# Part of w_ch and two row blocks of w_in decoded in another stage of a three-part kernel (attention, gated layer, rotation layer)

## The chip, the cores and the metric

One core of one Trainium2 chip. The metric is the device time of one execution in microseconds (us). The engines are TensorE (PE; its weight loads are PEld), VectorE (DVE), ScalarE (ACT), GpSimd (POOL) and SyncE (SP), which here issues all DMA transfers.

## The reference

Attention over 4 batches, 12 heads, 448 positions and 64 features a head, with the heads mixed before and after the softmax. Its output x, 4 x 448 x 768, goes through two layers:

```python
# layer one
h = gelu_tanh(x @ w_in)                       # 768 -> 1024
u, v = h[..., :512], h[..., 512:]
v_n = (v - mean(v)) / sqrt(var(v) + 1e-6) * g_ln
v_s = einsum('ts,bsd->btd', w_sg, v_n) + b_sg[None, :, None]
x = x + (u * v_s) @ w_out                     # 512 -> 768
# layer two
theta = x @ w_theta                           # 768 -> 768
y = einsum('ts,bsd->btd', w_tok_r, x * cos(theta)) + einsum('ts,bsd->btd', w_tok_i, x * sin(theta))
u = x + y
out = u + maximum(u @ w_ch, 0)                # 768 -> 768
```

## The kernel before

All matrix products of the layers are made of three: an fp32 operand is split into a high part (a ScalarE cast to the reduced type `fp32r`) and a low part (the operand minus that cast), and high x high, high x low and low x high are added up in PSUM. Activations are split when they are made. The weights w_in, w_out, w_theta, w_tok and w_ch lie in memory as 64-bit floats; the kernel decodes them from the two 32-bit words of each number into a high and a low part. That is the work that the change moves about.

**The decode.** One piece is 128 rows and 256 (or 192) columns. `Dense.decode` makes six steps of it: load the raw words; two ScalarE copies and two VectorE bit operations (`words`, L597 to L602); a VectorE mask (`value`, L608); a ScalarE cast and a VectorE product (`high`, L613, L614); a VectorE subtraction and a GpSimd addition (`low`, L620, L621); a store to a scratch tensor in memory (`store`, L627), unless the result goes straight into tiles. Pieces are made in two ways:

- `extra`: a list handed to `attention`, spread evenly over its 180 blocks: the v half of w_in (columns 512 to 1023, 12 pieces) and the u half of the first KE row blocks (2 pieces each), all stored to `win_d` and loaded again by `load_win`.
- `d.jobs`: a list worked off by `d.tick`, a software pipeline over the list: each tick makes one step of each of the pieces under way, so that a full tick is one piece's worth of work; the last step of a piece (its store) is seven ticks behind its load. The list is: the u half of w_in's remaining row blocks, straight into tiles (two pieces a block); w_out (12 pieces, tiles); w_theta (18), w_tok (14) and the first KC row blocks of w_ch (3 each), all by way of memory. Some ticks run beside the end of attention (`at(-6 + KE + i, d.tick)`), the others behind units of layer one, as many as the tables TV, TU, TG and TO say for the units `v_chunk`, `u_half`, `gate` and `out` of each batch. What is left runs in `rest` of layer two.

The row blocks of w_ch from KC on are decoded in layer two, in tiles of 128 x 384, without scratch memory: `load_wch` brings the raw words, `words_wch` makes a ScalarE copy and four VectorE operations, `split_wch` a ScalarE cast (high part), and two VectorE operations (low part).

**The order of the work.** Every engine works in order, and the order of emission is written out by hand. Attention is a loop over blocks of 10 positions x 12 heads (score matmuls, a layout change by DMA, the head mix on TensorE, a row maximum on VectorE, exp on ScalarE, split and normalisation on GpSimd and VectorE, the second head mix, its split, then the product with v and the transposed store to `xT`). v of each batch is scaled and split beside some of the blocks (L181, L184, L188). Behind the loop layers one and two are a list of units, each with work put before (`pre`) and behind it (`post`). For each batch layer one runs `v_chunk` (4 or 3), `out` of the batch before, `u_half` (4), `gate` (4). The first four `v_chunk` units run beside the end of attention. In layer two `theta` units (two a chunk of 128 positions, with `angles` and `rotate` behind them) come first, then six `tok` units of batch 0, then for each batch theta of the next, six `ch` units of the one before and six `tok`. `tok0` is the index of the first `tok` unit. The chunk (1, 0) is computed ahead of `tok0`, and its rotation is held back to the last `tok` units of batch 0.

A `tok` unit accumulates in one of eight PSUM buffers, VectorE adds x (L1117), ScalarE casts the sum to `uh`, and the difference makes `ul`; both feed the `ch` units.

Of the kernel before, what the change touches and what calls it, by code (L numbers as in the profile page):

```python
# [7 lines left out]
F32R = mybir.dt.float32r  # L8
# [475 lines left out]
NO2 = 3  # L484
TV = ((), (2, 2, 2), (1, 1, 1, 1), (1, 1, 1))
TU = ((2, 1, 1, 1), (2, 1, 1, 1), (2, 1, 1, 1), (1, 1, 1, 2))
TG = ((1, 0, 1, 0), (1, 0, 1, 0), (1, 0, 1, 0), (1, 1, 0, 0))
TO = ((1, 1, 1, 1, 1, 1), (1, 0, 1, 0, 1, 0), (1, 0, 1, 0, 1, 0), (0, 1, 1, 0, 0, 0))
KC = 3
KE = 1  # L490
MAGIC = 12582912.0
INV2PI = 1.0 / (2.0 * math.pi)
C1 = 6.28125
# [5 lines left out]
class Dense:  # L499
# [64 lines left out]
    def scratch(self, dram):  # L564
# [3 lines left out]
        self.wtok_d = t("wtok_d", 2 * S, S)  # L568
        self.wch_d = t("wch_d", 128 * KC, DM)

# [89 lines left out]
def moe1(d, left, right):  # L660

    tc, nc, io = d.tc, d.nc, d.io
# [4 lines left out]
    def start():  # L667
# [14 lines left out]
        pair = lambda pool, n, tag: [d.pools[pool].tile([128, n], F32R, tag=f"{tag}_{i}", name=tag) for i in range(2)]  # L682
        for k in range(KE, KD):
            def tiles(k=k):
                win[k, 0] = pair("win", HF, f"win{k}_0")
                return win[k, 0]
            d.jobs += d.decode_tiles(io["w_in"], slice(128 * k, 128 * k + 128), 0, HF, tiles)
        d.jobs += [None]
        for k in range(KF):
            def tiles(k=k):  # L690
# [4 lines left out]
                   + d.decode_all(io["w_tok"], 0, S, d.wtok_d)  # L695
                   + d.decode_all(io["w_ch"], 0, DM, d.wch_d, 128 * KC))

# [166 lines left out]
    for b in range(B + 1):  # L864
# [13 lines left out]
        if b < B:  # L878
            g0[b] = len(d.units)
            for f in range(KF):  # L880
                i = U(gate, b, f)
# [8 lines left out]
    for b in range(B):  # L890
# [3 lines left out]
        for c in range(nv):  # L894
            i = o0[b - 1][0] + 1 + c if b else u0[0] + c // 2
# [3 lines left out]
        if b + 1 < B:  # L899
            i = u0[b] + KF  # L900
# [9 lines left out]
    for b in range(B):  # L910
# [4 lines left out]
        for f in range(KF):  # L915
            ticks[u0[b] + f] = TU[b][f]
            ticks[g0[b] + f] = TG[b][f]
        for m in range(KD):
            ticks[o0[b][m]] = TO[b][m]
    for i, n in ticks.items():  # L920
# [4 lines left out]
    def at(s, fn, *a):  # L925
        tail.setdefault(s, []).append(lambda: fn(*a))
# [4 lines left out]
    for k in range(KD):  # L931
        at(-6 + k // 2, load_win, k, 1)
    for k in range(KE):
        at(-3, load_win, k, 0)
    for i in range(17 - 2 * KE):
        at(-6 + KE + i, d.tick)
    for c in range(4):
# [7 lines left out]
def moe2(d, left, win_es, last_u, m1_left):  # L945
    tc, nc, io = d.tc, d.nc, d.io
    wth, wch, wtok, z, x2, st, ut, res = ({} for _ in range(8))
# [23 lines left out]
    def load_wch(k, half):  # L971
        if k < KC:
            wch[k, half] = d.load_pair(d.pools["wch"], d.wch_d, slice(128 * k, 128 * k + 128),
                                       slice(384 * half, 384 * half + 384), f"wch{k}_{half}")
            return
        raw = d.pools["wch"].tile([128, 384, 2], U32, tag=f"wch{k}_{half}", name="wchraw")
        src = io["w_ch"][128 * k:128 * k + 128, 384 * half:384 * half + 384]
        nc.sync.dma_start(out=raw.rearrange("p n w -> p (n w)"), in_=src.bitcast(U32))
        wch[k, half] = raw

    def words_wch(k, half):
        raw = wch[k, half]
        a, p = (d.pools["t2"].tile([128, 384], F32, tag=f"zz{i}", name=f"ch{i}") for i in range(2))
        nc.scalar.activation(out=p, in_=raw[:, :, 1].bitcast(F32), func=AF.Copy, scale=2.0 ** -112)
        au, pu = a.bitcast(U32), p.bitcast(U32)
        nc.vector.tensor_scalar(out=au, in0=pu, scalar1=3, scalar2=0x7FFFFFF8,
                                op0=ALU.logical_shift_left, op1=ALU.bitwise_and)
        nc.vector.scalar_tensor_tensor(out=au, in0=pu, scalar=0x80000000, in1=au,
                                       op0=ALU.bitwise_and, op1=ALU.bitwise_or)
        nc.vector.tensor_scalar(out=pu, in0=au, scalar1=0xFF800000, scalar2=None, op0=ALU.bitwise_and)  # L990
        nc.vector.tensor_tensor(out=p, in0=p, in1=raw[:, :, 0], op=ALU.mult)
        st["ch", k, half] = a, p

    def split_wch(k, half):
        a, p = st.pop(("ch", k, half))
        t = d.pools["wch"].tile([128, 2, 384], F32R, tag=f"wch{k}_{half}", name="wch")
        d.cast(t[:, 0], a)
        d.rest(nc.vector, a, a, t[:, 0])
        nc.vector.scalar_tensor_tensor(out=t[:, 1], in0=p, scalar=2.0 ** -52, in1=a, op0=ALU.mult, op1=ALU.add)
        wch[k, half] = t[:, 0], t[:, 1]  # L1000
# [103 lines left out]
    def tok(b, k):  # L1104
        if k == 0:
            ut[b] = ([], [])
        fs = slice(128 * k, 128 * k + 128)
        ps = d.ps()
        terms = []
        for c in (0, 1, 2, 3) if b % 2 == 0 else (3, 0, 1, 2):  # L1110
            for ri in range(2 if c < 3 else 1):
                zh, zl = (z[(b, c, ri, hl) if c < 3 else (b, 3, hl)][:, fs] for hl in "hl")
                wh, wl = wtok[(c, ri) if c < 3 else 3]
                terms += [(zh, wh), (zh, wl), (zl, wh)]
        d.mm(ps[:, :S], terms)
        x = res.pop(("x", b, k))
        nc.vector.tensor_tensor(out=x, in0=ps[:, :S], in1=x, op=ALU.add)  # L1117
        uh, ul = (d.pools["x"].tile([128, 512], F32R, tag=f"x{i}{k}", name="u") for i in range(2))
        uh, ul = uh[:, :S], ul[:, :S]
        d.cast(uh, x)  # L1120
        d.rest(nc.gpsimd, ul, x, uh)
        ut[b][0].append(uh)
        ut[b][1].append(ul)

# [23 lines left out]
        for half in range(2):  # L1148
            d.post(last_u + 1 + k, load_wth, k, half)
    d.pre(first, rest)  # L1150
    chunks = []
    def theta_units(b, cs):
        for c in cs:
            chunks.append((b, c, len(d.units)))
            for half in range(2):
                U(theta, b, c, half)

    for b in range(B):
        cs = (0, 1, 2, 3) if b % 2 == 0 else (0, 1, 2)
        theta_units(b, cs if b != 1 else cs[1:])  # L1160
        if b == 0:
            theta_units(1, (0,))
        if b:
            for m in range(KD):
                U(ch, b - 1, m)
        k0 = len(d.units)
        if b == 0:
            tok0 = k0
        for k in range(KD):
            U(tok, b, k)  # L1170
        for k in range(KD):
            d.pre(k0 + k - 1, load_res, b, k)
# [10 lines left out]
    for i in range(7):  # L1183
        d.pre(first + 1 + i, load_wtok, i)
    words = [(k, half) for half in range(2) for k in range(KC, KD)]
    for j, kh in enumerate(words):
        d.pre(tok0 - 3 + j, load_wch, *kh)
        d.post(tok0 + j, split_wch, *kh)
    for j, kh in enumerate(words):
        d.post(tok0 - 1 + j, words_wch, *kh)  # L1190
    for half in range(2):
        for k in range(KC):
            d.pre(tok0 + k + half, load_wch, k, half)
# [13 lines left out]
def build(tc, nc, io, out):  # L1207
    with tc.manual_schedule(), ExitStack() as top:
        dram = top.enter_context(tc.tile_pool(name="scratch", bufs=1, space=bass.MemoryType.DRAM))
        xT = dram.tile([DM, B * S], F32, name="xT")  # L1210
        x2T = dram.tile([DM, B * S], F32, name="x2T")
        d = Dense(tc, nc, io, xT, x2T, out)
        d.scratch(dram)
        right, left1, left2 = ExitStack(), ExitStack(), ExitStack()
        tail, win_es, last_u, end = moe1(d, left1, right)
        th_es = moe2(d, left2, win_es, last_u, left1)
        for i in range(4):
            tail.setdefault(-2 + 2 * i, []).append(d.step)
        jobs = d.decode_all(io["w_in"], HF, DFF, d.win_d)
        jobs += d.decode_all(io["w_in"], 0, HF, d.win_d, 128 * KE)  # L1220
        attention(tc, nc, io, xT, B, jobs, tail)
        while d.at < len(d.units):
            d.step()
        th_es.close()
        right.close()
        left2.close()
# [54 lines left out]
```

## Time and profile before

| | |
|---|---|
| median of 3 runs | 1026.55 us (1026.28 to 1028.11) |
| profiled execution | 1026.51 us, span of its instructions 1024.7 us |
| TensorE busy | 975.8 us, 95% of the span, granted clock 0.985 on average |
| TensorE weight loads | 742.4 us, 72% |
| VectorE busy | 784.0 us, 77% |
| ScalarE busy | 593.3 us, 58% |
| GpSimd busy | 483.6 us, 47% |

The columns of a busy table are the sum of an engine's busy time in a stretch, the number of its instructions in brackets, the clock granted to TensorE as a share of full speed, the busy share of the DMA engines and what they moved. In a timeline a row is: start, length, engine, line of the kernel, operation, output <- input, shapes, how many in a row, and in square brackets how long the engine was idle just before and who ended that. A row of waits is: who <- for whom, microseconds in total, how often, the longest.

### The profile page before, as it was taken

To read this page: it belongs to the slowest core of one execution; us is meant where nothing else is said; L and a number is where in the kernel's file an instruction comes from. 1 tells how busy PE (TensorE), PEld (TensorE's weight loads), DVE (VectorE), ACT (ScalarE), POOL (GpSimd) and SP (SyncE) were. 2 spreads that over 40 slices of the span, in tenths; PEclk is the share of its full clock that TensorE was granted. 3 is DMA by queue.
4 is the path that set the end of the run, shared out by engine and by line. 5 is a ranking of instruction groups with operands and counts; after the bars stand their busy time and mean duration, and the time that the engine had idled before them with its cause. 6 is when DMAs were issued, how large, how long until landed. Compare 5 with 4: busy or idle time off the path is not lost.

```text
span 1024.7 us, 21768 instructions
## 1 busy us (share of the span) xinstructions
PE 975.8 (95%) x7856; PEld 742.4 (72%) x7856; DVE 784.0 (77%) x1605; ACT 593.3 (58%) x1392; POOL 483.6 (47%) x653
## 2 busy tenths in 40 slices
PE   8889999999999999997998999999997899999998
PEld 3456565566656565576877888888987799999997
DVE  2999879988889888986999898984987825835511
ACT  5777788688877887765855646442552513513310
POOL 0694458655685557752312222222552643743623
PEclk9999999999999999998999999999999899999999
DMA  5557555654456445248534856679761031130121
GB/s 172 184 180 216 142 147 176 190 152 141 149 194 206 133 156 172 101 108 277 181 99 148 264 180 207 205 241 287 228 218 49 17 109 31 32 108 16 39 70 54
DMA packets 126905, 153.17 MB, mean 149 GB/s; under 512 B 26318, under 2 KB 113230, under 8 KB 126798
## 3 DMA queue, kind: packets, MB, share of 16 engines
q1 hardware_dynamic: 126798, 151.78, 47.4%
q8 instruction: 63, 1.03, 0.4%
q14 instruction: 44, 0.36, 0.1%
HBM read 82.73 MB, written 30.47 MB: 110 GB/s over the span
## 4 chain that ended last, share of the span: by engine, by line
PE 70%; DVE 17%; DMA 4%; ACT 3%; issue 3%; POOL 2%; SPq 1%; DVEq 0%; ACTq 0%; POOLq 0%
PE ps L562 39%; PE psB L226 10%; PE psA L206 6%; PE psD L332 5%; DVE pl L265 3%; PE psC L280 3%; PE psC L283 2%; PE psC L281 2%; DVE al L311 2%; DVE nmx L232 2%; DMA blk<-s 1%; DMA win<-win_d 1%; DVE dp L608 1%; DMA x2T<-xres 1%; DVE dp L614 1%
## 5 line engine op out<-in xcount | busy, mean ns | idle before, releaser
L258 POOL TENSOR_SCALAR ph<-e,rc 120x448 f16<-120x448 f32 x180 | 174.2, 968 | 145.3 <-DVE rc L253 94.6
L226 PE MATMUL psB<-blk,kpre 120*120 120x448 f32 x360 | 175.2, 569 | 5.1 <-DMA blk<-s 2.9
L232 DVE TENSOR_REDUCE nmx<-psB 120x1 f32<-120x448 f32 x180 | 111.2, 618 | 43.5 <-PE psB L226 42.7
L265 DVE SCALAR_TENSOR_TENSOR pl<-e,rc,ph 120x448 f16<-120x448 f32 x180 | 143.2, 796 | 0.0
L239 ACT ACTIVATE e<-psB,nmx 120x448 f32<-120x448 f32 x180 | 114.2, 634 | 36.7 <-DVE nmx L232 34.7
L311 DVE SCALAR_TENSOR_TENSOR al<-psC,ah 128x480 f16<-128x480 f32 x180 | 116.1, 645 | 7.6 <-ACT ah L305 7.0
L562 PE MATMUL ps<-wtok,z 128*128 128x448 f32 x504 | 104.3, 367 | 0.4 <-POOL z L558 0.4
L212 ACT ACTIVATE s<-psA 120x896 f32<-120x896 f32 (+1 forms) x90 | 82.4, 916 | 37.5 <-PE psA L206 36.0
L305 ACT ACTIVATE ah<-psC 128x480 f16<-128x480 f32 x180 | 103.1, 573 | 0.1
L562 PE MATMUL ps<-wth,x2s 128*128 128x384 f32 x504 | 96.3, 348 | 6.9 <-DVE xres L1117 4.2
L280 PE MATMUL psC<-wh,ph 120*128 120x120 f16 x720 | 96.9, 218 | 6.1 <-DVE rc L253 4.1
L562 PEld LDWEIGHTS ps<-wtok,z 128*128 128x128 f32 x504 | 94.5, 188 | 9.5 <-POOL z L558 0.8
L621 POOL TENSOR_TENSOR dh<-da,dp 128x256 fp32r<-128x256 f32 (+1 forms) x55 | 44.7, 813 | 119.8 <-DVE da L620 70.4
L280 PEld LDWEIGHTS <-ph 120*128 120x128 f16 x720 | 68.3, 98 | 42.5 <-POOL rc L247 18.3
L332 PEld LDWEIGHTS <-ah 128*128 128x128 f16 x1536 | 76.6, 99 | 30.6 <-issue 30.6
L206 PE MATMUL psA<-k,q 64*120 64x448 f32 (+1 forms) x384 | 96.2, 580 | 1.0 <-ACT s L212 1.0
L562 PEld LDWEIGHTS ps<-wth,x2s 128*128 128x128 f32 x504 | 91.0, 195 | 8.3 <-DVE xres L1117 4.1
L281 PE MATMUL psC<-wl,ph 120*128 120x120 f16 x720 | 96.1, 217 | 0.0
L562 PE MATMUL ps<-u,wch 128*128 128x448 f32 x432 | 89.5, 367 | 0.0
L562 PEld LDWEIGHTS ps<-u,wch 128*128 128x128 f32 x432 | 81.1, 188 | 7.6
L558 POOL TENSOR_TENSOR z<-zz,z 128x384 fp32r<-128x384 f32 x56 | 61.9, 1125 | 47.0 <-ACT z L555 46.8
L332 PE MATMUL psD<-vh,ah 128*128 128x64 f16 x768 | 78.6, 195 | 0.0
(132 smaller groups left out, 2071.4 us busy)
## 6 DMA issues: line engine op xcount, KB each, us to landing
blk<-s SPq DMA_DIRECT2D x176, 210.0 KB
draw<-in_w_in SPq DMA_DIRECT2D x24, 256.0 KB
vraw<-in_vN SPq DMA_DIRECT2D x24, 256.0 KB
k<-in_kvT SPq DMA_DIRECT2D x24, 224.0 KB
vT<-in_kvT SPq DMA_DIRECT2D x12, 448.0 KB
xraw<-xT SPq DMA_DIRECT2D x24, 224.0 KB
xres<-xT SPq DMA_DIRECT2D x24, 224.0 KB
x2T<-xres SPq DMA_DIRECT2D x24, 224.0 KB
```

Of the source, the lines that this page charges most:

```text
L206: nc.tensor.matmul(ps[e][:n, :S], q[p, o:o + n], k[p], start=True, stop=True)
L226: nc.tensor.matmul(ps[:r, :S], kpre[:r, :r], sblk.pop(s)[:r], start=True, stop=True)
L232: nc.vector.tensor_reduce(out=m[:r], in_=mix[s][:r, :S], axis=AX.X, op=ALU.max, negate=True)
L239: nc.scalar.activation(out=e[:r], in_=mix.pop(s)[:r, :S], func=AF.Exp, bias=nmx.pop(s)[:r], accum_out=sm[:r])
L258: nc.gpsimd.tensor_scalar(out=p[:r], in0=ex[s][0][:r], scalar1=rec[s][:r], scalar2=0.0, op0=ALU.mult, op1=ALU.add)
L265: nc.vector.scalar_tensor_tensor(out=p[:r], in0=ex.pop(s)[0][:r], scalar=rec.pop(s)[:r], in1=ph[s][:r], op0=ALU.mult, op1=ALU.subtract)
L280: nc.tensor.matmul(ps[:, jc, :, :n], cols(a, jc), wh[:r, :, :n], start=(jc == 0), stop=False)
L281: nc.tensor.matmul(ps[:, jc, :, :n], cols(a, jc), wl[:r, :, :n], start=False, stop=False)
L305: nc.scalar.activation(out=at_view(s, at[b, t][0]), in_=src, func=AF.Copy, scale=2.0 ** -17)
L311: nc.vector.scalar_tensor_tensor(out=al, in0=src, scalar=2.0 ** -17, in1=ah, op0=ALU.mult, op1=ALU.subtract)
L332: nc.tensor.matmul(ps[:, o:o + 64], a[:, i0:i0 + 128], v[:, jc, 64 * e:64 * e + 64], start=(o == 0 and m == 0), stop=(o == 320 and m == le ...
L562: self.nc.tensor.matmul(ps, l, r, start=(i == 0), stop=(i == len(terms) - 1))
```

## The change

Two constants and three tables change, and the order of the work on w_ch in layer two:

- KE goes from 1 to 3: the u half of two more row blocks of w_in (4 pieces) is decoded beside attention's blocks, 18 pieces instead of 14, and goes by way of memory; the list `d.jobs` loses these 4 pieces, and 11 ticks instead of 15 run beside the end of attention. The three blocks are loaded at steps 1 to 3 behind attention's last block.
- KC goes from 3 to 4: one more row block of w_ch (3 pieces) is decoded in `d.jobs`; layer two decodes two row blocks, 4 tiles instead of 6, spread over the units from tok0 - 1 to tok0 + 5.
- TG and TO have four ticks more: behind the last `gate` of batch 0, behind `out` units of batches 2 and 3.
- In layer two the cast of w_ch's high part is emitted with the words, directly behind them, and no longer with the split one unit later.
- u's low part is computed by VectorE and no longer by GpSimd.

```diff
-TG = ((1, 0, 1, 0), (1, 0, 1, 0), (1, 0, 1, 0), (1, 1, 0, 0))
-TO = ((1, 1, 1, 1, 1, 1), (1, 0, 1, 0, 1, 0), (1, 0, 1, 0, 1, 0), (0, 1, 1, 0, 0, 0))
-KC = 3
-KE = 1
+TG = ((1, 0, 1, 1), (1, 0, 1, 0), (1, 0, 1, 0), (1, 1, 0, 0))
+TO = ((1, 1, 1, 1, 1, 1), (1, 0, 1, 0, 1, 0), (1, 0, 1, 0, 1, 1), (0, 1, 1, 1, 1, 0))
+KC = 4
+KE = 3
...
     for k in range(KE):
-        at(-3, load_win, k, 0)
+        at(1 + k, load_win, k, 0)
     for i in range(17 - 2 * KE):
         at(-6 + KE + i, d.tick)
...
         nc.vector.tensor_tensor(out=p, in0=p, in1=raw[:, :, 0], op=ALU.mult)
-        st["ch", k, half] = a, p
-
-    def split_wch(k, half):
-        a, p = st.pop(("ch", k, half))
         t = d.pools["wch"].tile([128, 2, 384], F32R, tag=f"wch{k}_{half}", name="wch")
         d.cast(t[:, 0], a)
+        st["ch", k, half] = a, p, t
+
+    def split_wch(k, half):
+        a, p, t = st.pop(("ch", k, half))
         d.rest(nc.vector, a, a, t[:, 0])
...
         d.cast(uh, x)
-        d.rest(nc.gpsimd, ul, x, uh)
+        d.rest(nc.vector, ul, x, uh)
...
     for j, kh in enumerate(words):
-        d.pre(tok0 - 3 + j, load_wch, *kh)
-        d.post(tok0 + j, split_wch, *kh)
-    for j, kh in enumerate(words):
-        d.post(tok0 - 1 + j, words_wch, *kh)
+        i = tok0 - 1 + (3 * j + 1) // 2
+        d.pre(i - 2, load_wch, *kh)
+        d.post(i + 1, split_wch, *kh)
+        late_words.append((i, kh))
+    for i, kh in late_words:
+        d.post(i, words_wch, *kh)
```

## Rows read from the trace of the kernel before

**Rows 1.** Busy time by stage; stretch, length, then the engines.
```profile
20.00:468.00 448.00, 430.56 (x5047) 261.71 (x5047) 394.08 (x823) 354.34 (x861) 282.80 (x452) 1.00 0.54 163
...
480.00:550.00 70.00, 62.98 (x431) 52.62 (x430) 66.75 (x154) 47.79 (x122) 16.98 (x20) 0.96 0.44 136
...
550.00:700.00 150.00, 148.03 (x684) 127.99 (x682) 132.60 (x305) 77.36 (x180) 34.76 (x41) 0.99 0.69 224
762.00:800.00 38.00, 28.18 (x139) 25.62 (x137) 29.50 (x52) 10.64 (x22) 9.13 (x9) 0.89 0.11 33
...
830.00:1025.00 195.00, 191.12 (x987) 177.91 (x985) 85.50 (x139) 48.44 (x98) 83.18 (x75) 1.00 0.18 56
```

**Rows 2.** Whom TensorE waited for, from 440 us to the end.
```profile
PE ps L562 <- POOL wout L621: 3.1, 1, 3.1
...
PE ps L562 <- DVE x L558: 2.1, 2, 1.4
...
PE psT L345 <- ACT xi L336: 1.7, 1, 1.7
```

**Rows 3.** Timeline of the first tok stage, 764 to 802 us.
```profile
766.83 0.62 DVE L1117 TENSOR_TENSOR xres<-ps,xres 128x448 f32<-128x448 f32 x1
...
768.45 0.56 ACT L555 ACTIVATE u<-xres 128x448 fp32r<-128x448 f32 x1
...
783.57 0.62 DVE L1117 TENSOR_TENSOR xres<-ps,xres 128x448 f32<-128x448 f32 x1
784.22 0.58 ACT L555 ACTIVATE u<-xres 128x448 fp32r<-128x448 f32 x1 [3.78 <-DVE xres L1117]
...
784.24 4.96 PE L562 MATMUL ps<-wth,x2s 128*128 128x384 f32 x18 [3.83 <-DVE xres L1117]
784.70 0.51 ACT L555 ACTIVATE wch<-ch 128x384 fp32r<-128x384 f32 x1
784.87 1.15 POOL L558 TENSOR_TENSOR u<-xres,u 128x448 fp32r<-128x448 f32 x1 [4.08 <-ACT u L555]
...
785.24 1.20 DVE L558 TENSOR_TENSOR ch<-ch,wch 128x384 f32<-128x384 f32 x1 [1.06 <-ACT wch L555]
786.47 0.56 DVE L999 SCALAR_TENSOR_TENSOR wch<-ch,ch 128x384 fp32r<-128x384 f32 x1
786.95 0.35 DVE L986 TENSOR_SCALAR ch<-ch 128x384 uint32<-128x384 uint32 x1
...
788.79 0.62 DVE L1117 TENSOR_TENSOR xres<-ps,xres 128x448 f32<-128x448 f32 x1
...
797.87 0.55 DVE L1094 TENSOR_TENSOR zz<-ps,r 128x384 f32<-128x384 f32 x1
...
798.51 0.87 PE L1056 MATMUL ps<-ident,x 128*128 128x128 f32 x3 [3.25 <-issue]
...
800.50 1.97 PE L562 MATMUL ps<-wth,x2s 128*128 128x384 f32 x5 [1.11 <-DVE r L1070]
```

**Rows 4.** Timeline of VectorE around 501 us: one step of two pieces.
```profile
500.71 0.42 DVE L620 TENSOR_TENSOR da<-da,win 128x256 f32<-128x256 f32 x1
...
502.80 0.42 DVE L620 TENSOR_TENSOR da<-da,win 128x256 f32<-128x256 f32 x1
```

**Rows 5.** Busy time of two stretches behind waits of TensorE.
```profile
500.00:506.00 6.00, 4.77 (x18) 4.29 (x19) 5.90 (x16) 5.97 (x19) 2.57 (x3) 0.72 0.56 173
...
546.00:556.00 10.00, 7.43 (x29) 6.81 (x30) 9.83 (x24) 6.31 (x14) 3.62 (x5) 0.83 0.55 181
```

**Rows 6.** Whom TensorE waited for in attention, 20 to 468 us.
```profile
PE psC L283 <- DVE pl L265: 5.1, 11, 0.8
PE psC L280 <- DVE rc L253: 4.1, 6, 2.1
```

**Rows 7.** Timeline of VectorE at the end of layer one.
```profile
694.77 0.63 DVE L558 TENSOR_TENSOR g<-gt,g 128x448 fp32r<-128x448 f32 x1 [5.31 <-ACT g L555]
...
718.12 0.62 DVE L857 TENSOR_TENSOR xres<-ps,xres 128x448 f32<-128x448 f32 x1 [1.03 <-DMA xres<-xT]
```

More of the change, by code (lines that the diff above doesn't have):

```diff
@@ L1150, in moe2 @@
     d.pre(first, rest)
-    chunks = []
+    chunks, late_words = [], []
     def theta_units(b, cs):
```

## The prediction, made before the changed kernel ran

> **What bounds the kernel now.** I read first the table of busy time by stage [rows 1]. In attention (20 to 468 us) TensorE is busy 430.56 of 448 us and VectorE 394.08; from 550 to 700 TensorE has 148.03 of 150, after 830 it has 191.12 of 195. So TensorE sets the time there. Two stretches are different: from 480 to 550 VectorE is busy 66.75 of 70 us and TensorE 62.98, and from 762 to 800 TensorE has only 28.18 of 38 us, at a granted clock of 0.89. There VectorE sets the pace. Then I read whom TensorE waits for [rows 2] and, for the second hole, the timeline [rows 3]; the rest are prices.
>
> **The second hole (the first `tok` stage).** The six `tok` units of batch 0 each end in a VectorE add, L1117. The first add starts at 766.83, and in the middle of the stage the adds are 5.22 us apart (783.57 to 788.79) [rows 3]. TensorE is done with these matmuls long before and stands still for want of PSUM buffers: 3.83 us before the matmuls at 784.24, 3.25 before the transposes at 798.51, 1.11 before the matmuls at 800.50. One VectorE period is: add (783.57), ScalarE casts u (784.22) and then w_ch's high part (784.70), VectorE waits 1.06 us for that, takes the rest (785.24, 1.20 us long) and the second low-part operation (786.47), then the four operations on words (from 786.95 to the next add, 1.84 us). The changed stage has two such jobs less, but a VectorE subtraction for u's low part in all six units. I lay it out with the same rows:
> - Add, ScalarE's cast, subtraction: 0.65 us from the add to the cast (783.57 to 784.22), 0.58 of cast, 0.05 to start: the subtraction starts 1.28 after the add. I price the subtraction at 0.53 (a 448-column add is 0.62 long, and here VectorE starts its next operation some 0.09 before the end, 786.47 plus 0.56 against 786.95). That is 1.81 per unit, 10.9 for six.
> - A split pair: before 785.24 to 786.95, 1.71. The first of the two is 1.20 long while GpSimd's subtraction for u (784.87, 1.15 us) runs beside it; the second, with none beside it, 0.56. With u's low part no longer on GpSimd I take 1.06 for the pair, four times: 4.2.
> - Words: the first of the four jobs runs before 766.83, as now; three remain, 5.5.
> - The first unit's cast comes late behind the angles (768.45, that is 0.97 after it could): 1.0.
>
> Sum 21.6, so rotation of the held-over chunk would start at 788.4, where it starts at 797.40 now (0.47 before its second operation at 797.87): 9.0 us sooner. The transposes at 798.51 and the matmuls at 800.50 wait for exactly this rotation and the angles behind it, so TensorE gets there 9.0 us sooner if it has nothing else to wait for. From 780.41 (784.24 less the 3.83) it has two units of at most 4.96 and half the transposes to do, so it arrives by 791 at the latest, about when VectorE releases it. Both ends: 9.0 if the laid-out order holds; 3.4 if the contention stays in all four split pairs (0.65 each, 2.6) and ScalarE's early cast of w_ch, which waits in order for four VectorE operations and has u's cast queued behind it, costs each unit another 0.5 (3.0). I take 9.0, since VectorE's last word operation ends before the add that u's cast needs.
>
> A rule of the Trainium skill speaks against moving work here: Perfetto Trace Analysis, Optimizing Scalar/DVE Operations, says that because GpSimd and VectorE share a port, offloading between those two might not help. By that rule the 0.65 saved in the pair and the 0.53 spent cancel, and the trace does show the 1.20 beside the 0.56 [rows 3]; then nearly all of the 9.0 comes from the two jobs left out, which is how the sum above has it as well.
>
> **The first hole (end of attention, start of layer one).** The list of decodes that the first layer makes itself has four w_in pieces fewer at its head, and four ticks fewer run beside the end of attention. When VectorE is full a piece takes 2.09 us (500.71 to 502.80) [rows 4], so VectorE is 8.4 us further on in this stretch. The last piece of w_out was the 28th tick's and is now the 24th's; before the first `out` unit 25 ticks run, where there were 28. What it removes:
> - TensorE's 1.7 us wait for the attention output copy, xi [rows 2], which ScalarE makes behind decode casts that wait for VectorE. The copy itself stays, so I take 1.1. After this wait the clock is 0.72 over 6 us [rows 5]: 1.7 us lost, which I count as gained.
> - The waits for split x, 2.1 [rows 2]: gone, as VectorE is 8.4 ahead and TensorE by then 2.8.
> - The wait for w_out, 3.1 [rows 2]: TensorE arrives 4.9 sooner, the piece up to 8.4; VectorE then waits for `v_chunk` itself, so 1.0 stays and 2.1 is gained. Clock 0.83 over the 10 us there [rows 5]: 1.7.
>
> Sum 8.7. Bounds: 2.8 (xi and its clock alone) to 10.3 (all three waits and both clock stretches). It is kept through 550 to 700, where TensorE is full and VectorE at 132.60 of 150 [rows 1].
>
> **Attention.** Four decodes more run there, 18 for 14: on VectorE five operations, 2.09 uncontended, with three on ScalarE and one on GpSimd, and 0.5 MB of transfers each. TensorE covers them wherever it sets the pace. With 14 decodes it waited 9.2 us for VectorE (5.1 for pl, 4.1 for rc) [rows 6], 0.66 a decode; four more cost 2.6 by that. Bounds: nothing, if the 54 us in which VectorE idles [rows 1] take them, and 8.4, if none does. I take 2.6. Loading the two added w_in blocks, 0.5 MB each, comes after the split of x and while TensorE is on `v_chunk`; they take the place of as many bytes of raw words, so nothing.
>
> **The end of layer one.** One more block of w_ch is three more pieces, and two more full ticks' worth of VectorE work, 4.2 us, falls among the last `out` units. VectorE has idle time there but can't use it: in-order it stands 5.31 us behind the cast of g (694.77), and the last residual add (718.12) waits for its load, which waits for an earlier store [rows 7]. All of layer two's VectorE chain starts behind that add. SP issues two more stores ahead of it. Between 0 (all inside the wait for loads) and 4.2; I take 2.5, the 1.1 by which the words delay the first of these adds and 1.4 for the stores.
>
> **Nothing:** u's low part in batches 1 to 3. VectorE is busy 85.50 of 195 us there and TensorE 191.12 [rows 1]; were that cover gone, it is 18 times 1.8. Loading two more w_ch tiles takes the place of two raw ones of the same size.
>
> The profiled execution took 1026.51 us (span 1024.7), the median of the runs shown is 1026.55, so the sum stands against either: 1026.5 - 9.0 - 8.7 + 2.6 + 2.5 = 1013.9. I forecast **1014**.
>
> **The rivals.**
> - *Attention pays (slower).* The added decodes fall in the three stretches in which v is prepared and GpSimd is busy. If each of an added decode's operations takes twice its time, as 1.20 for 0.56 in [rows 3], it is 4.4 us, and if TensorE's clock falls behind it each time, 1.7 more [rows 5]: 6.1 for 0.66, four times, 22 us: 1036. It decides against the kernel once an added decode costs above 3.8 us (15.2 over four). For it: 0.66 is a mean over decodes of which most met no wait. Against it: the longest wait for VectorE is 2.1 [rows 6]. Chance 0.07. SBUF — State Buffer, Who interferes with whom, of the Trainium skill has the mechanism: of GpSimd and VectorE the second to issue blocks until the first is done, and this trace agrees with its 1.20.
> - *The second layer's gain is mostly lost:* ScalarE's early cast holds u's, contention stays: 3.4 for 9.0, 1019.5. Chance 0.14.
> - *The first layer's gain does not come:* VectorE's 8.4 us are eaten by waits for raw words or for the loads of w_in from memory, and the same three waits stay: 1022.6. Chance 0.12.
> - *All extra work is hidden:* no 2.6, no 2.5, and a little more at the first hole: 1007. Chance 0.10.
> - *The work only moves:* as many decodes are made as before, and what one hole gains another stretch pays: 1026. Chance 0.05.
>
> **How the numbers follow.** The forecast has 0.52, with its own range 1009 to 1019 (attention 0 to 8, or the end of layer one 0 to 4). The range 1005 to 1023 takes in the forecast, the second, third and fourth rival: 0.88. A difference of 0.2% (2 us) is about what a measurement of this kernel can tell. Faster by more: 0.52 + 0.14 + 0.10 + 0.10 of the third = 0.86. Same: 0.05 + 0.02 = 0.07. Slower: 0.07.
>
> **What would show it.** Right: from the first L1117 of batch 0 to the rotation some 21.6 us instead of 30.6, the L558 on w_ch near 0.55 us, no TensorE wait for L1117; no wait for w_out above 1 us and none for x; attention's end later by at most 3 us. Wrong: waits for pl or rc well above 9.2 us; a wait for L1117 that stays; ScalarE idle before u's cast for over 4 us a unit; the last residual add of layer one late by more than 4 us against TensorE.

## The result, and the profile after

The changed kernel takes 1017.98 us (median, 1016.67 to 1018.47); the kernel before, beside it on the same chip, 1026.97. Ratio 0.9914, 95% interval 0.9900 to 0.9928. The profiled execution took 1016.67 us with a span of 1014.9. The forecast was 1014, and 1017.98 is 4 above it: the gain is 9.0 us by medians and 9.8 by the two profiled executions, where 12.6 were forecast.

Where it came from is read from TensorE's timeline. The table has the starts of units in us from the start of each trace. The difference is counted from the first matmul of the second head mix that reads pl (L283), at 26.1 us before and 25.1 after, so 1.0 is taken off; plus means that the changed kernel is later.

| first matmul of | before | after | difference | forecast at this point |
|---|---|---|---|---|
| block 170 of attention, second mix | 453.1 | 452.8 | +0.7 | +2.6 |
| v_chunk(0,0) | 470.8 | 471.2 | +1.4 | |
| v_chunk(0,1) | 482.0 | 480.3 | -0.7 | |
| u_half(0,0) | 501.5 | 499.1 | -1.4 | |
| v_chunk(1,0) | 528.1 | 524.2 | -2.9 | |
| v_chunk(1,1) | 535.1 | 530.0 | -4.1 | |
| out(0,0) | 543.2 | 538.2 | -4.0 | |
| u_half(1,0) | 555.5 | 550.4 | -4.1 | -6.1 |
| out(3,0) | 696.0 | 691.2 | -3.8 | -6.1 |
| first theta | 713.5 | 711.5 | -1.0 | |
| tok0 | 750.0 | 748.7 | -0.3 | -3.6 |
| theta(1,2), second half | 800.5 | 790.2 | -9.3 | -12.6 |
| last ch | 1017.2 | 1006.9 | -9.3 | -12.6 |

The spans differ by 9.8: the 9.3, 1.0 by which the first mix starts earlier in the after trace, less 0.5 at its end.

The busy table of the changed kernel, stretches as in [rows 1], set some 1 us (10 in layer two) earlier:

```profile
479.00:549.00 70.00, 64.47 (x443) 54.63 (x443) 63.85 (x147) 45.36 (x117) 15.10 (x18) 0.98 0.50 154
...
820.00:1015.00 195.00, 190.81 (x983) 177.19 (x981) 96.75 (x157) 48.44 (x98) 62.38 (x57) 1.00 0.18 55
```

At 480 to 550 VectorE is 2.9 us less busy than in [rows 1]. Behind 820 it has 11 us more to do and TensorE is as full as before.

Whom TensorE waits for in the changed kernel from 440 us on, beside [rows 2]:

```profile
PE psC L280 <- DVE al L311: 3.4, 2, 1.8
PE ps L562 <- DVE g L558: 3.4, 3, 2.2
PE ps L562 <- POOL wout L621: 3.1, 1, 3.1
PE ps L1056 <- issue: 2.6, 1, 2.6
...
PE ps L562 <- DVE r L1070: 1.5, 1, 1.5
PE ps L562 <- DVE x L558: 1.3, 1, 1.3
PE psT L345 <- ACT xi L336: 1.1, 1, 1.1
PE ps L562 <- DMA win<-win_d: 1.0, 3, 0.5
```

The waits for the residual add (L1117) are gone, xi is at 1.1, x fell by 0.8 only, and w_out is where it was. A wait of 2.2 for g is new (the longest was 1.0), and the wait for al, the low part of the mixed heads in attention's last two blocks, is 3.4 where it was 1.9.

The first tok stage in the changed kernel's timeline, beside [rows 3]:

```profile
765.50 0.61 DVE L1117 TENSOR_TENSOR xres<-ps,xres 128x448 f32<-128x448 f32 x1
...
779.01 0.62 DVE L558 TENSOR_TENSOR u<-xres,u 128x448 fp32r<-128x448 f32 x1 [0.64 <-ACT u L555]
779.55 0.55 DVE L558 TENSOR_TENSOR ch<-ch,wch 128x384 f32<-128x384 f32 x1
...
780.62 0.62 DVE L1117 TENSOR_TENSOR xres<-ps,xres 128x448 f32<-128x448 f32 x1
...
787.14 0.55 DVE L1094 TENSOR_TENSOR zz<-ps,n 128x384 f32<-128x384 f32 x1
...
788.25 0.52 PE L1056 MATMUL ps<-ident,x 128*128 128x128 f32 x3 [2.58 <-issue]
790.23 3.13 PE L562 MATMUL ps<-wth,x2s 128*128 128x384 f32 x9 [1.46 <-DVE r L1070]
```

From the first add to the rotation are 21.64 us (765.50 to 787.14), as summed (21.6). L558 on w_ch takes 0.55 and has no wait ahead of it.

VectorE at the start of layer one, rows ahead of which it had been idle, first in the kernel before and then in the changed one:

```profile
476.50 0.29 DVE L600 TENSOR_SCALAR da<-dp 128x256 uint32<-128x256 uint32 x1 [3.77 <-ACT dp L597]
...
482.21 0.69 DVE L768 BATCH_NORM_STATS2 bst<-v 128x6 f32<-128x512 f32 x1 [1.48 <-ACT v L763]
```

```profile
479.89 0.69 DVE L768 BATCH_NORM_STATS2 bst<-v 128x6 f32<-128x512 f32 x1 [4.94 <-ACT v L763]
485.30 0.69 DVE L768 BATCH_NORM_STATS2 bst<-v 128x6 f32<-128x512 f32 x1 [1.95 <-ACT v L763]
490.51 0.69 DVE L768 BATCH_NORM_STATS2 bst<-v 128x6 f32<-128x512 f32 x1 [0.98 <-ACT v L763]
496.13 0.69 DVE L768 BATCH_NORM_STATS2 bst<-v 128x6 f32<-128x512 f32 x1 [0.57 <-ACT v L763]
```

That is 8.4 us in which VectorE stands, in order, ahead of `v_chunk`'s statistics (L768), for the v that TensorE and ScalarE make. Before, it stood 1.9 us there, and 5.0 for the raw words of two pieces (L600). In all, it idles 12.6 of the 40 us up to its split of w_sg (504.59), and idled 8.6 of the 40 before (up to 509.63).

The end of layer one in the changed kernel, beside [rows 7]:

```profile
691.40 0.83 DVE L600 TENSOR_SCALAR da<-dp 128x256 uint32<-128x256 uint32 x1
692.27 0.43 DVE L602 SCALAR_TENSOR_TENSOR da<-dp,da 128x256 uint32<-128x256 uint32 x1
692.61 0.68 DVE L829 SCALAR_TENSOR_TENSOR gt<-ps,gln,bsg 128x448 f32<-128x448 f32 x1
...
694.53 0.88 PE L562 MATMUL ps<-g,wout 128*128 128x448 f32 x3 [2.16 <-DVE g L558]
```

Two operations on words (L600, L602) now stand ahead of gate's own at 692.61, and TensorE waits 2.16 us for the g that comes of it. The granted clock of 690 to 700 is 0.88, a mean of the two levels, 1.2 and 2.4 GHz:

```profile
690.00:700.00 10.00, 6.61 (x25) 5.12 (x24) 9.83 (x21) 3.50 (x9) 1.79 (x2) 0.88 1.08 341
```

### The profile page after: what moved, and what is told of

It is laid out like the page before. It is cut to its first block, busy times and chain, and to the rows that moved or that the text cites. A ratio compares the mean times of both kernels' runs of the same rounds, so it can differ in the third digit from the quotient of the medians.

```text
span 1014.9 us, 21794 instructions
## 1 busy us (share of the span) xinstructions
PE 971.0 (96%) x7856; PEld 738.8 (73%) x7856; DVE 792.0 (78%) x1632; ACT 595.7 (59%) x1397; POOL 462.5 (46%) x632
## 4 chain that ended last, share of the span: by engine, by line
PE 74%; DVE 16%; ACT 3%; issue 2%; DMA 2%; POOL 2%; SPq 0%; DVEq 0%; ACTq 0%; POOLq 0%
PE ps L562 40%; PE psB L226 11%; PE psA L206 7%; PE psD L332 6%; PE psC L280 3%; PE psC L283 3%; PE psC L281 3%; DVE pl L265 3%; DVE al L311 2%; DVE nmx L232 1%; DMA win<-win_d 1%; PE psT L345 1%; DVE r L1071 1%; DVE dp L608 1%; DMA blk<-s 1%
## 5 line engine op out<-in xcount | busy, mean ns | idle before, releaser
L258 POOL TENSOR_SCALAR ph<-e,rc 120x448 f16<-120x448 f32 x180 | 178.1, 990 | 140.1 <-DVE rc L253 88.6
L621 POOL TENSOR_TENSOR dh<-da,dp 128x256 fp32r<-128x256 f32 (+1 forms) x62 | 50.5, 815 | 121.2 <-DVE da L620 88.9
L562 PE MATMUL ps<-wth,x2s 128*128 128x384 f32 x504 | 93.8, 341 | 3.5 <-POOL x2s L558 2.0
L558 POOL TENSOR_TENSOR z<-zz,z 128x384 fp32r<-128x384 f32 x56 | 61.9, 1127 | 73.4 <-ACT z L555 73.3
L562 PEld LDWEIGHTS ps<-wth,x2s 128*128 128x128 f32 x504 | 88.5, 190 | 4.5 <-POOL x2s L558 2.6
L332 PEld LDWEIGHTS <-al 128*128 128x128 f16 x768 | 68.3, 98 | 12.8 <-issue 12.8
```

Source lines behind the costliest of these rows:

```text
L258: nc.gpsimd.tensor_scalar(out=p[:r], in0=ex[s][0][:r], scalar1=rec[s][:r], scalar2=0.0, op0=ALU.mult, op1=ALU.add)
L332: nc.tensor.matmul(ps[:, o:o + 64], a[:, i0:i0 + 128], v[:, jc, 64 * e:64 * e + 64], start=(o == 0 and m == 0), stop=(o == 320 and m == le ...
L562: self.nc.tensor.matmul(ps, l, r, start=(i == 0), stop=(i == len(terms) - 1))
```

## The experiments

Each is compared with the kernel before on the same chip (its medians there: 1026.61 to 1026.77). "Changed" is the changed kernel; starts of units are again taken from the first mix of their own trace.

**1 and 2. Each half alone.** The changed kernel without the w_in blocks, and the kernel before with them:

```diff
-KE = 3
+KE = 1
...
-        at(1 + k, load_win, k, 0)
+        at(-3, load_win, k, 0)
```

> The changed kernel with KE = 1, so that w_in is decoded as before and only w_ch and layer two change. Theory A: the first tok stage gains the same 9.0 us, the waits at the start of layer one (xi 1.7, x 2.1, w_out 3.1) are those of before, and the end of layer one costs 2.5 to 3: the run is 6 us below before, near 1021. Rival B (w_in's part gives nothing that reaches the end): the run equals the changed kernel, near 1018.

Measured 1022.06 us, ratio 0.9954 (0.9941 to 0.9967).

```diff
-KE = 1
+KE = 3
...
-        at(-3, load_win, k, 0)
+        at(1 + k, load_win, k, 0)
```

> The kernel before with KE = 3 and the three loads at steps 1 to 3; w_ch, layer two and the tick tables as before. Theory A: TensorE is 4 us ahead at the start of layer one (out of batch 0) as in the changed kernel, nothing is lost at the end of layer one, and as VectorE's chain into the first tok stage begins 4 us earlier the run ends 3 to 4 us below before, near 1023.5. Rival B: what TensorE gains in layer one is waited off again in the first tok stage, which VectorE sets: within 1 us of before, 1026 to 1027. Rival C (the prediction's 8.7 less attention's 2.6): near 1021.

Measured 1023.47 us, ratio 0.9968 (0.9955 to 0.9980). Theory A holds in both, though the first gains less than its 6: the halves are worth 4.6 and 3.2 us, together 7.8 of the changed kernel's 9.0, and the 1.2 between lies inside the intervals. In w_in alone the end of layer one is as before (17.6 us from out(3,0) to the first theta, 17.5 before) and the waits for L1117 stay; in w_ch alone the tok stage has its gain (21.7 us from the first add to the rotation) and the end of layer one takes 20.5. The loss at the end of layer one belongs to w_ch's ticks.

**3. u's low part on GpSimd again.**

```diff
-        d.rest(nc.vector, ul, x, uh)
+        d.rest(nc.gpsimd, ul, x, uh)
```

> The changed kernel with u's low part on GpSimd again, all else as changed. Theory A (VectorE's list of work sets the first tok stage): without the six subtractions and the six waits of 0.64 us for u's cast, the stretch from the first L1117 to the rotation falls from 21.6 to between 13 us (no contention) and 15.5 us (each of four rests 1.2 us long beside GpSimd); TensorE then no longer waits for the rotation (2.6 us) nor for the angles (1.5) and keeps its clock there, so the run is 4 to 5.5 us below the changed kernel, near 1013. Rival B (the gain comes from taking u's low part away from GpSimd and with it the contention): the run is above the changed kernel by 2 to 3 us, near 1020.5.

Measured 1015.62 us, ratio 0.9895 (0.9883 to 0.9908): the direction of A, half its size. Its interval overlaps the changed kernel's a little. Its timeline in the tok stage:

```profile
766.51 0.62 DVE L1117 TENSOR_TENSOR xres<-ps,xres 128x448 f32<-128x448 f32 x1
...
773.32 0.56 DVE L558 TENSOR_TENSOR ch<-ch,wch 128x384 f32<-128x384 f32 x1
773.91 1.55 DVE L999 SCALAR_TENSOR_TENSOR wch<-ch,ch 128x384 fp32r<-128x384 f32 x1
...
786.99 0.54 DVE L1094 TENSOR_TENSOR zz<-ps,n 128x384 f32<-128x384 f32 x1
```

The stage takes 20.48 us for 21.64. Six subtractions of 0.62 and the 0.64 waited for ScalarE ahead of most of them are gone from VectorE, but the operation beside GpSimd's subtraction takes 1.55 where it took 0.56, and ahead of two of the pieces VectorE waits 1.09 us for ScalarE's copy of the words (L984). The contention had only moved from L558 to the next operation, so the expected 13 to 15.5 us were wrong.

**4. The cast of w_ch's high part in the split again.**

```diff
         t = d.pools["wch"].tile([128, 2, 384], F32R, tag=f"wch{k}_{half}", name="wch")
-        d.cast(t[:, 0], a)
         st["ch", k, half] = a, p, t
...
         a, p, t = st.pop(("ch", k, half))
+        d.cast(t[:, 0], a)
```

> The changed kernel, with the high part of w_ch cast by ScalarE in the split again and not with the words; everything else as changed. Theory A (VectorE sets the pace of the first tok stage and stands 1.06 us behind that cast for each piece, as in the kernel before): up to four times 1.06 us longer, the stage 23 to 26 us instead of 21.6, 1020 to 1022. Theory B (the subtraction for u's low part now stands between the add and the split, so the cast is done by then): no difference, 1017 to 1018.5.

Measured 1018.18 us, ratio 0.9916 (0.9903 to 0.9929): no difference, B. The subtraction for u, which now stands ahead, gives ScalarE the time for either cast:

```profile
773.60 0.62 DVE L558 TENSOR_TENSOR u<-xres,u 128x448 fp32r<-128x448 f32 x1 [0.65 <-ACT u L555]
774.14 0.55 DVE L558 TENSOR_TENSOR ch<-ch,wch 128x384 f32<-128x384 f32 x1
```

**5. Three late ticks put earlier.** From behind out(2,5), out(3,3) and out(3,4) to behind the last gates of batches 1 and 2 and out(1,5), in TG and TO, the two tables that the change itself touches:

```diff
-TG = ((1, 0, 1, 1), (1, 0, 1, 0), (1, 0, 1, 0), (1, 1, 0, 0))
-TO = ((1, 1, 1, 1, 1, 1), (1, 0, 1, 0, 1, 0), (1, 0, 1, 0, 1, 1), (0, 1, 1, 1, 1, 0))
+TG = ((1, 0, 1, 1), (1, 0, 1, 1), (1, 0, 1, 1), (1, 1, 0, 0))
+TO = ((1, 1, 1, 1, 1, 1), (1, 0, 1, 0, 1, 1), (1, 0, 1, 0, 1, 0), (0, 1, 1, 0, 0, 0))
```

> The changed kernel with the three ticks that it has behind the last out units of batches 2 and 3 moved into batches 1 and 2 (one behind the last out of batch 1, one behind the last gate of batches 1 and 2). Theory A: at the end of layer one TensorE's wait for g falls from 3.2 back to 2 us without loss of clock, VectorE's chain of layer two begins 2 to 3 us earlier, and the run is 2 to 3 us below the changed kernel, near 1015.5. Rival B (the cost is not the ticks' place but the number of stores and the bytes at the end of layer one, or the middle of layer one becomes VectorE's): the run is within 1 us of the changed kernel or above it.

Measured 1022.94 us, ratio 0.9962 (0.9948 to 0.9977): B. The end of layer one is short again (17.4 us), but in this kernel's timeline g is late three times before it:

```profile
602.18 5.32 PE L562 MATMUL ps<-g,wout 128*128 128x448 f32 x25 [1.01 <-DVE g L558]
655.48 0.89 PE L562 MATMUL ps<-g,wout 128*128 128x448 f32 x3 [1.69 <-DVE g L558]
658.80 6.36 PE L562 MATMUL ps<-g,wout 128*128 128x448 f32 x19 [2.44 <-DVE g L558]
```

**6. No tick behind gate(3,1).** It goes to out(3,0):

```diff
-TG = ((1, 0, 1, 1), (1, 0, 1, 0), (1, 0, 1, 0), (1, 1, 0, 0))
-TO = ((1, 1, 1, 1, 1, 1), (1, 0, 1, 0, 1, 0), (1, 0, 1, 0, 1, 1), (0, 1, 1, 1, 1, 0))
+TG = ((1, 0, 1, 1), (1, 0, 1, 0), (1, 0, 1, 0), (1, 0, 0, 0))
+TO = ((1, 1, 1, 1, 1, 1), (1, 0, 1, 0, 1, 0), (1, 0, 1, 0, 1, 1), (1, 1, 1, 1, 1, 0))
```

> The changed kernel, with the decode tick behind gate(3,1) moved to out(3,0), so that the two VectorE operations on words no longer stand ahead of gate's own VectorE operations at 692.6. Theory A (this tick is what delays g: TensorE's waits for g of 2.16 and 1.03 with a clock of 0.93 behind them, 20.3 us from out(3,0) to the first theta matmul where it was 17.5): the wait for g is back near 1, the stretch near 17.5 to 18, about 1015.2 us, 2 to 3 below the changed kernel. Theory B (the two added ticks behind out(3,3) and out(3,4) delay the last residual add): the stretch stays near 20, 1017 to 1019.

Measured 1016.09 us, ratio 0.9894 (0.9878 to 0.9910). That is 1.9 below the changed kernel, whose interval it overlaps, so the trace has to decide, and it is for A: 16.8 us from out(3,0) to the first theta, for 20.3. Busy table and TensorE's rows:

```profile
690.00:700.00 10.00, 8.57 (x40) 7.00 (x39) 7.64 (x15) 3.27 (x7) 0.91 (x1) 1.00 1.09 357
```

```profile
694.78 0.88 PE L562 MATMUL ps<-g,wout 128*128 128x448 f32 x3 [0.21 <-DVE g L558]
696.69 0.88 PE L562 MATMUL ps<-g,wout 128*128 128x448 f32 x3 [1.03 <-DVE g L558]
```

One wait of 2.16 is gone and the clock behind it whole. The same ticks behind out(3,3) and out(3,4) are still there, so they were not the cause of this wait.

**7. The ticks beside attention's end begin two steps earlier.**

```diff
-        at(-6 + KE + i, d.tick)
+        at(-5 + i, d.tick)
```

> The changed kernel, with the eleven decode ticks beside the end of attention begun at step -5 of its tail, as before the change, and not at -3. In the changed kernel VectorE idles 4.94, 1.95, 0.98 and 0.57 us in order behind v_chunk's statistics (L768), and TensorE still waits 3.15 us for w_out. Theory A (four ticks less did not put VectorE 8.4 us ahead, because half of the time it saved became this idle time): two more pieces of 2.09 us run in those gaps, VectorE is up to 4 us further on, the wait for w_out falls from 3.15 to 1 or less with the half clock behind it, the waits for x go: about 1014 us, 3 to 4.5 below the changed kernel's 1018. Theory B (the raw words or the loads of w_in arrive too late for that, so an earlier tick only waits): no difference, 1017 to 1019, the wait for w_out near 3.

Measured 1018.52 us, ratio 0.9930 (0.9915 to 0.9946): no gain, B. Its waits, 440 to 720 us:

```profile
PE ps L562 <- DMA win<-win_d: 4.0, 4, 1.9
...
PE ps L562 <- POOL wout L621: 3.2, 1, 3.2
```

The gaps ahead of `v_chunk`'s statistics are filled, as A said: 1.7 us are left of the 8.4. But VectorE now waits for raw words that land late, as in the kernel before:

```profile
476.98 0.29 DVE L600 TENSOR_SCALAR da<-dp 128x256 uint32<-128x256 uint32 x1 [3.24 <-ACT dp L597]
```

With 1.1 us more ahead of the next piece, it idles 12.0 of the 40 us up to its split of w_sg, for 12.6, and is only 0.6 us further on there. So w_out stays at 3.2, as B had it. TensorE's waits for the loads of w_in are 4.0 us (1.0 in the changed kernel). Their sum moves by itself, from 0.5 to 2.8 us in the nine traces that have KE = 3 and the changed kernel's first tick. But a single wait of 1.8 to 2.2 us stands in all three traces whose ticks begin at step -5 (before, w_ch alone and this one), and the longest in the other ten is 1.5: with raw words asked for earlier, v_chunk's weights land later.

**8. w_out decoded by column blocks.**

```diff
+        blocks = []
         for k in range(KF):
...
-            d.jobs += d.decode_tiles(io["w_out"], slice(128 * k, 128 * k + 128), 0, DM, tiles)
+            blocks.append(d.decode_tiles(io["w_out"], slice(128 * k, 128 * k + 128), 0, DM, tiles))
+        d.jobs += [block[c] for c in range(DM // 256) for block in blocks]
```

> The changed kernel, with the twelve pieces of w_out decoded column block by column block instead of row block by row block, so that the first out units need 4 of the 12. Same work, same number of pieces and ticks. Theory A (the 3.15 us wait at out(0) is for VectorE's progress through the list of decodes): the wait for w_out and the half clock behind it go, 3 to 4.5 us less, about 1014; the waits for xi (1.1) and x (1.3) stay. Theory B (TensorE would there be held by something else that ends at the same time, such as the split x or the statistics): the wait only changes its name, 1017 to 1018.5.

Measured 1018.45 us, ratio 0.9924 (0.9909 to 0.9938). From this kernel's timeline:

```profile
540.09 6.23 PE L562 MATMUL ps<-g,wout 128*128 128x448 f32 x30
...
585.07 0.73 PE L562 MATMUL ps<-win,x 128*128 128x512 f32 x2 [1.64 <-ACT x L555]
587.39 12.95 PE L562 MATMUL ps<-win,x 128*128 128x512 f32 x49 [1.59 <-DVE x L558]
```

The wait for w_out is gone (A), and TensorE gets 5.0 us from out(0,0) to u_half(1,0) (7.3 us for 12.3). Around 585 it gives all of it back, waiting for the split x of the third batch and at a lower clock behind it: 29.8 us from v_chunk(2,0) to u_half(2,0) for 23.8, at a granted clock of 0.94 for 1.00. The time is B's; neither theory had both.

**9. The same, and the third batch's x ahead of three ticks.** They move from behind out(0,3), out(0,4) and out(0,5) to behind v_chunk(2,0), v_chunk(2,1) and v_chunk(2,2):

```diff
-TV = ((), (2, 2, 2), (1, 1, 1, 1), (1, 1, 1))
+TV = ((), (2, 2, 2), (2, 2, 2, 1), (1, 1, 1))
...
-TO = ((1, 1, 1, 1, 1, 1), (1, 0, 1, 0, 1, 0), (1, 0, 1, 0, 1, 1), (0, 1, 1, 1, 1, 0))
+TO = ((1, 1, 1, 0, 0, 0), (1, 0, 1, 0, 1, 0), (1, 0, 1, 0, 1, 1), (0, 1, 1, 1, 1, 0))
```

> The changed kernel with w_out decoded by column blocks, as in the run before, which took the wait for w_out away and got waits for x of 1.64 and 1.59 us at 583 us for it; and now also with the three ticks behind out(0,3) to out(0,5) moved behind v_chunk(2,0) to v_chunk(2,2), so that the split of the third batch's x is not behind them on VectorE. Theory A (VectorE, busy without a gap from 497 to 586 us, sets the time of this stretch; three pieces of 2.09 us less in front of x let TensorE keep the 3 to 5 us): the waits for x at 583 go, about 1014 us, 3.5 to 5 below the changed kernel, if VectorE catches up before the splits of g. Theory B (VectorE has no room behind either): waits for g of 1 to 3 us come up between 600 and 660, 1017 to 1020.

Measured 1019.09 us, ratio 0.9928 (0.9912 to 0.9944): B. TensorE is 3.0 us ahead of the changed kernel at u_half(2,0) and 0.4 behind it at v_chunk(3,0). A wait of 1.50 for x is still there ahead of the first, and one of 1.67 for vnm comes between the two:

```profile
583.86 13.47 PE L562 MATMUL ps<-win,x 128*128 128x512 f32 x58 [1.50 <-DVE x L558]
630.02 0.96 PE L562 MATMUL ps<-wsg,vnm 128*128 128x448 f32 x2 [1.67 <-DVE vnm L558]
```

The late operand is now the norm of v (vnm), where g was expected: another name for the same lack.

**10. All six row blocks of w_in beside attention.**

```diff
-KE = 3
+KE = 6
```

> The changed kernel with all six row blocks of the first half of w_in decoded beside attention (KE 6 for 3): six decodes more there, six ticks fewer beside its end. Theory A (attention hides a decode at 0.2 to 0.7 us each, as the change's four cost 0.75 us together; and the start of layer one gains nothing from still fewer ticks, because VectorE then only idles behind v_chunk and the ticks of w_out can't begin sooner): attention's end 1 to 4 us later, the waits for w_out and x the same, 1018.5 to 1022. Theory B (each piece less puts VectorE 2.09 us ahead there, up to 12.5): the waits for x and w_out go, 1012 to 1015. Theory C (attention has no room left: 2 us or more for a decode): above 1026.

Measured 1022.64 us, ratio 0.9963 (0.9949 to 0.9977): nearest to A, 0.6 above its range. Waits of this kernel from 440 to 720 us:

```profile
PE ps L562 <- POOL wout L621: 3.2, 1, 3.2
...
PE ps L562 <- DVE x L558: 0.8, 1, 0.8
```

Attention's block 170 is 5.3 us later than in the changed kernel for six decodes (A had 1 to 4), and layer one gains nothing for it.

**11. Experiments 3 and 6 together.**

> The changed kernel with two edits together: no tick behind gate(3,1) (1016.1 alone, 1.9 below the changed kernel) and u's low part on GpSimd as before (1015.6 alone, 2.4 below). Theory A (they act in different stretches, the end of layer one and the first tok stage, and add): 1013 to 1014.5. Theory B (after layer one VectorE's rotation sets the pace up to 790 us, and what one edit gains the other can't use): 1015 to 1016.5.

Measured 1014.07 us, ratio 0.9874 (0.9862 to 0.9887): they add (A). It is the fastest version here, 3.9 us below the changed kernel by medians where the two alone are 2.4 and 1.9, and its interval doesn't touch the changed kernel's.

## Why the prediction was right, and where it was not

The direction and the larger part of the size were right. The four terms, forecast and measured from the table of starts: first tok stage -9.0 and -9.0; attention +2.6 and +0.7; start of layer one -8.7 and -4.8; end of layer one +2.5 and +3.8 (from u_half(1,0) to tok0).

**First tok stage: right, by the sum that was laid out.** The gain comes from the two tiles less: each had 1.84 of words, 1.71 of split and 1.06 of waiting in [rows 3], 4.6, twice 9.2. The two other edits in that stage are worth little, each taken out alone: the early cast nothing (experiment 4), u's low part on VectorE about 1 us to the bad in the stage (experiment 3: 1.16 us shorter without it). No run takes out both; by the rows, the 30.57 us of the stage before less 9.2 would be 21.4, an estimate. The sum's 1.06 for a split pair had the contention wholly gone (1.71 less 0.65), and so it is: 1.07 (779.55 to 780.62, the next operation). But the subtraction and the wait ahead of it, six times, cost about 1 us more than leaving it on GpSimd. The Trainium skill (Perfetto Trace Analysis, Optimizing Scalar/DVE Operations) says that offloading between GpSimd and VectorE might not help. Experiment 3 agrees: 20.48 us with the subtraction on GpSimd, 21.64 on VectorE.

**Start of layer one: the term that was mis-sized.** It was forecast at 8.7 us and measured 4.8. The step that failed is "VectorE is 8.4 us further on in this stretch", with the three waits then summed. Two signs that the prediction named for being right did not come: no wait for w_out above 1 us (it is 3.1) and none for x (1.3). What the runs showed:
- Of the 8.4, about half became idle time (12.6 us for 8.6, above): the remaining eleven ticks begin two steps later, and VectorE stands in order ahead of `v_chunk`'s statistics. Its split of w_sg (L558) ran at 509.63 before and at 504.59 after, 1.0 of which is the shift of the trace: 4.0 us ahead.
- xi gave 0.6, the wait going from 1.7 to 1.1, where 1.1 was to be gained. The lower clock behind it ([rows 5], 0.72) is gone, as forecast: 1.00 from 499 to 505 us.
- 2.1 us came from a place that the sum left out, TensorE's waits for the loads of w_in (v_chunk(0,0) to (0,1) 9.1 us for 11.2). Experiment 7 points to the cause: with raw words loaded two steps earlier the long wait is there again. The size is less certain: in the nine traces with this order the stretch is 8.6 to 10.2 us, in the two with the old one 10.8 and 11.2.
- 0.7 us was lost ahead of v_chunk(0,0), where the wait for al grew. The second of its two waits is 1.1 to 1.8 us in all ten traces with KE = 3 and 0.3 with KE = 1 and 6; why is open.
- x and w_out can't be summed. Both are VectorE's work, in order. A lead of VectorE shortens the wait for x, which comes first; TensorE then gets to w_out sooner by as much as the piece is earlier, and waits as long as before. In every trace with w_out decoded by rows its wait is 3.0 to 3.2, whether x is 2.1 (before), 1.3 (changed) or 0.8 (experiment 10). From the end of the last wait for x to the end of the wait for w_out it is 14.4 to 14.6 us in all eleven, with VectorE idle for at most 0.4 us between. Two rows of TensorE before, and two of the changed kernel:

```profile
534.02 9.37 PE L562 MATMUL ps<-win,x 128*128 128x512 f32 x40 [1.40 <-DVE x L558]
...
548.57 3.72 PE L562 MATMUL ps<-g,wout 128*128 128x448 f32 x11 [3.14 <-POOL wout L621]
```

```profile
528.97 9.37 PE L562 MATMUL ps<-win,x 128*128 128x512 f32 x40 [1.29 <-DVE x L558]
...
543.51 3.05 PE L562 MATMUL ps<-g,wout 128*128 128x448 f32 x8 [3.15 <-POOL wout L621]
```

- And much more would not have been kept. I wrote that a gain is "kept through 550 to 700", because TensorE is full there and VectorE has 17 us to spare. For the 4 us that came, this holds (-4.1 at u_half(1,0), -3.8 at out(3,0)). But the spare time is not where more would need it: 5.0 us gained at out(0,0) came back as waits for x at 585 (experiment 8) and for vnm at 630 (experiment 9), and three pieces moved in there made g late (experiment 5). In the changed kernel VectorE is busy 80.69 of the 86 us from 500 to 586.

**Attention: 0.66 a decode holds, if the clock is counted apart; that it came out cheaper is luck.** In the kernel before one wait of 2.05 us at 181 us has a granted clock of 0.97 behind it over 176 to 234 us; the changed kernel has waits of 0.45, 1.41 and 0.31 there and a clock of 1.00, worth about 1.5 us (51.9 for 53.5 from block 60 to 80). Counted without it the four decodes cost 2.2. Experiment 6 has the same decodes and the same waits there, but a clock of 0.97, and is 2.8 us later than the kernel before at block 170, so the 1.5 is not the change's own. That the waits alone did not set the clock is shown at the end. Six more (experiment 10, clock 0.97 again) cost 5.3 us, less the 1.5 of the clock: 3.8, or 0.63 each. The changed kernel's waits for VectorE in attention, beside [rows 6]:

```profile
PE psC L283 <- DVE pl L265: 7.4, 15, 1.4
PE psC L280 <- DVE rc L253: 4.2, 8, 1.4
```

**End of layer one: the size nearly right, the place wrong.** I put it at the last residual add, behind loads and stores. That add comes at 714.81 and VectorE waits for TensorE there. What cost was a tick that the change doesn't touch, the one behind gate(3,1): before, the list was at its end there and the tick had no words left (its L620, L614 and L608 run from 695.31, with gate's operation right behind them at 696.18); with three pieces more it is full, ahead of the VectorE operations on g. Experiment 6 moved that tick alone and had 3.5 us of this stretch back. Some of it was lost again in layer two, where 39.4 us pass from the first theta to tok0, for 37.2: a wait of 0.67 for x2s at 732 that the changed kernel doesn't have, and behind a later one of 2.00, which it has too, a clock of 0.89 from 735 to 750 where it had been 1.00.

Open: the 2.6 and 1.5 us that TensorE still waits at 788 and 790 in the changed kernel. Experiment 11 has 0.3 left of the first; no run took the 1.5 away.

## What to carry to other kernels

Waits of one engine for another that stand one behind the other on that engine are one wait: until the first is gone, a lead shortens only the first and the rest keep their length, so it is counted once. An engine with idle time in a stretch has room only where the idle time lies in front of an operand that is late; ask what an operation taken out leaves behind, idle time in order or a lead. When a list of work gets longer, look at the slots that used to run empty at its end: they fill first, wherever they stand.

## What the hardware did that was not expected

- The same waits were followed by different clocks. TensorE waited 0.45, 1.41 and 0.3 us around 180 us in the changed kernel and in experiment 6; the granted clock of 176 to 234 us was 1.00 in the one and 0.97 in the other, and block 60 to 80 took 51.9 and 53.5 us. A gain of 1.5 us in one profiled execution can be this alone. The first row is of the changed kernel, the second of experiment 6:

```profile
176.00:234.00 58.00, 55.64 (x651) 33.59 (x650) 52.61 (x109) 45.64 (x107) 37.09 (x60) 1.00 0.60 176
```

```profile
176.00:234.00 58.00, 55.59 (x634) 33.63 (x632) 51.81 (x109) 44.19 (x105) 35.98 (x56) 0.97 0.57 172
```

- A VectorE operation beside a GpSimd subtraction took 1.20 to 1.55 us for 0.56, whichever of three it was (L558 in [rows 3], L988 and L999 in experiment 3): among these, the loss goes with the GpSimd instruction, not with the VectorE one. The Trainium skill (SBUF — State Buffer, Who interferes with whom) says that a VectorE instruction with two SBUF inputs contends with a GpSimd instruction that reads SBUF. The rows agree in size: 1.55 is 0.56 and about 1 of GpSimd's 1.15.
